# Transposing three of four normalised token groups by DMA, and running three partial products over twelve token blocks instead of eight

## The chip, the core and the metric

The kernel runs on one core of one Trainium2 chip. The time is that of the device for one execution, in microseconds, from runs without a profiler; the median of three was 243.69 (242.27 to 244.08). A profile is one separate execution, recorded by the hardware: its span goes from the first to the last instruction. Engines are named as in the profile: PE (TensorE; PEld are its weight loads), DVE (VectorE), ACT (ScalarE), POOL (GpSimd) and SP (SyncE, which here only issues DMAs). Each engine works through its own list of instructions in order, and an instruction that waits holds up all that stand behind it on the same engine.

## What is computed

```python
def _A_ref(x, wqkv, wo):                      # x: 1 x 2048 x 512
    # 32 heads of 16; every query sees itself and the 255 tokens before it
    ...
    scores = jnp.where(mask[None, None], scores, -1000000000.0)
    p = _softmax(scores, axis=-1)
    o = jnp.einsum('bhqk,bhkd->bhqd', p, v)
    return (lambda x, *d: x.transpose(*d))(o, 0, 2, 1, 3).reshape(B, S, D) @ wo

def _B_ref(x, w1, b1, w2, b2):                # mixes tokens: 2048 -> 1792 -> 2048
    h = _layernorm(x, axis=-1)
    u = jnp.einsum('bsd,sf->bdf', h, w1) + b1
    u = _gelu(u)
    y = jnp.einsum('bdf,fs->bds', u, w2) + b2
    return (lambda x, *d: x.transpose(*d))(y, 0, 2, 1)

mod = (_silu(c) @ w_mod).reshape(c.shape[0], 6, 1, -1)   # sa, ca, ga, sb, cb, gb
h = _layernorm(x, axis=-1) * (1 + ca) + sa
x = x + ga * _A_ref(h, A_wqkv, A_wo)
h = _layernorm(x, axis=-1) * (1 + cb) + sb
x = x + gb * _B_ref(h, B_w1, B_b1, B_w2, B_b2)
```

All tensors are bf16. The sums of the products are f32.

## The kernel before

The 2048 tokens are cut into 16 blocks of 128 (`tb`), and these into 4 groups of four blocks (`tg`). The program has three stretches.

**Attention.** A group's four blocks are normalised (`st1`, `e1`, `r1`, `ap1`: statistics, then `xn1`, 128 tokens x 512), turned so that the 512 channels lie on the partitions (tile `h1T`, 128 x 4 x 512 tokens), and scaled and shifted by the modulation on the way. From `h1T` PE makes K, Q and V (`Kk`, `Qq`, `V`; one of these is a group of four matmul steps with N = 512, cut into quadrants at some places). A slab `s` (0 to 15) is eight heads of one token group; its scores come in units (76 in all, `S0` to `S75`; four for each slab of the first token group, five for the others). PE computes a unit's scores into two PSUM tiles, and ACT takes the exponential of each tile (`E`, two for each unit, 152 in all, line 868). Then PE multiplies by V (`P`), DVE turns the result back (`turn`, line 899), POOL divides (`merge`, line 912) and DVE turns once more (`back`, line 921). `Wo` is the output projection, after which two layer norms (`s2` to `m2`, `s3` to `p3`) make `hb`, the input of the mixer, one tile for each token block.

**The mixer's first product.** It has 14 column chunks of 128 (`fc`), each a sum over the 16 token blocks. For the twelve chunks in `PART` the first eight blocks are summed during the attention, where PE has room between units (`B0` to `B11`, eight steps each), and the partial sum is copied to SBUF (`part`); the other eight blocks follow once the attention is over (`U`, eight steps; `A` adds the partial sum, `G` is the gelu on ACT). Chunks 12 and 13 do all sixteen steps in `U`. The weights `w1` of blocks 0 to 7 are loaded during the attention (tile `w1a`), those of blocks 8 to 15 when the attention's buffers have been released (`reopen`, tile `w1b`, eight DMAs).

**The mixer's second product** (line 1451) is a sum over the 14 chunks for each of the 16 output blocks, with its evictions and the stores of the output.

In the kernel before, a group is turned by PE: `T1`, `T2` and `T3` are two groups each of eight 128 x 128 transposes (line 1142) into a PSUM bank, and DVE evicts them with scale and shift (line 1155, four instructions for each token group). Token group 0 is turned by PE in both kernels (line 688).

What stands in which order on each engine is set by a planner in the kernel (class `Order`): it has a list of tasks with engine, estimated cost, dependencies and buffers, walks through time, and takes on each engine the ready task of lowest rank. The table `PLACES` shifts ranks task by task, `BY` says which engine does a task that several could do, and `PATIENCE` says how far PE may run a block of other work past the moment at which the next unit should start. A score unit needs two of three PSUM tiles, and everything else on PE shares two banks. All DMAs but two are issued from SP in one order; one DMA reuses the semaphore of the DMA that was issued eight earlier, and its issue waits until that one has landed.

Of the kernel before, what the change touches and what calls it, by code (L numbers as in the profile page):

```python
# [1501 lines left out]
```

## Time and profile before

| | |
|---|---|
| median of three runs | 243.69 us (242.27 to 244.08) |
| the profiled execution's own time | 242.86 us |
| its span, first to last instruction | 241.1 us |
| granted TensorE clock | 1.000 |
| matmul instructions on PE | 4316 |
| HBM read, written | 22.55 MB, 2.10 MB |
| mean DMA rate over the span | 117 GB/s |

The profiled execution took 0.83 us less than the median of the runs, and 1.76 us of its time lie outside the span. In the views that follow, a row of the timeline gives the start, the duration, the engine, the line, the operation, the output and its inputs, the count, and in brackets the engine's idle time before it and what ended that. Rows of equal instructions are merged, and a row can be one or two matmuls short. In a row of the windows the engines' busy times stand one after the other, each with its number of instructions, then the granted clock, the DMA engines' busy share and the rate.

### The profile page before, as it was taken

The numbers are of one execution on the slowest core, as the hardware profiler recorded it, in microseconds if no ns is written. First come the engines' busy times: TensorE is split into PE (matmuls) and PEld (weight loads), VectorE is DVE, ScalarE is ACT, GpSimd is POOL, SyncE is SP. The second block draws the span as 40 slices with busy tenths as digits, with TensorE's granted clock in tenths as the row PEclk, the third lists the DMA queues.
The fourth block names the chain that finished last, engine by engine and source line by source line (L and its number), as shares of the span: only waits on it lengthen the run. The fifth ranks groups of instructions, "written<-read, shape, count | busy, mean of one in ns | idle before, by whom it ended". The sixth has DMA issues, their size and how long they took to land.

```text
span 241.1 us, 9843 instructions
## 1 busy us (share of the span) xinstructions
PE 229.8 (95%) x4316; PEld 118.4 (49%) x4358; DVE 177.3 (74%) x422; ACT 162.0 (67%) x188; POOL 95.1 (39%) x148
## 2 busy tenths in 40 slices
PE   7899899999999999999999999999999999999994
PEld 2545546555555554454454455454444444444443
DVE  8899998878999899999356867989964306060644
ACT  7599989999999999999999999900436400000000
POOL 5219675741655466996310113686920000000000
PEclk9999999999999999999999999999999999999999
DMA  5998713062260343210110110059999001111121
GB/s 157 306 346 245 223 30 122 18 177 59 60 188 5 73 113 73 82 35 4 35 38 10 29 38 3 3 183 387 411 406 411 35 0 46 44 44 44 44 91 44
DMA packets 26151, 28.09 MB, mean 117 GB/s; under 512 B 10488, under 2 KB 23292, under 8 KB 26108
## 3 DMA queue, kind: packets, MB, share of 16 engines
q1 hardware_dynamic: 25956, 27.33, 36.0%
q8 instruction: 34, 0.56, 1.0%
q10 hardware_dynamic: 152, 0.13, 0.2%
q14 instruction: 9, 0.07, 0.1%
HBM read 22.55 MB, written 2.10 MB: 102 GB/s over the span
## 4 chain that ended last, share of the span: by engine, by line
PE 69%; DVE 16%; DMA 5%; issue 3%; SPq 3%; POOL 2%; ACT 1%; DVEq 0%; ACTq 0%
PE bk L606 17%; PE pss L1451 15%; PE bk L890 7%; PE pss L606 6%; PE pss L847 6%; PE bk L610 6%; PE bk L1451 5%; DVE stats L599 4%; DMA w1b<-in_B_w_dram 3%; DMA wqkv<-in_A_wqkv_dram 2%; DVE t L899 2%; PE pss L859 2%; PE pss L819 2%; PE pss L828 1%; DVE QR L740 1%
## 5 line engine op out<-in xcount | busy, mean ns | idle before, releaser
L868 ACT ACTIVATE et<-pss 128x1024 bf16<-128x1024 f32 x152 | 141.7, 1050 | 1.8 <-PE pss L859 1.6
L1451 PEld LDWEIGHTS <-w2r 128*128 128x128 bf16 x238 | 23.1, 98 | 25.6
L912 POOL TENSOR_TENSOR merge<-t,zr 128x512 bf16<-128x512 f32 x16 | 16.9, 1057 | 32.5 <-DVE zr L908 32.4
L1460 DVE SCALAR_TENSOR_TENSOR o<-pss,bFM,bc_gb 128x512 bf16<-128x512 f32 (+2 forms) x13 | 8.8, 705 | 27.9 <-PE pss L1451 27.9
L1451 PE MATMUL pss<-guT,w2r 128*128 128x512 bf16 (+2 forms) x128 | 28.1, 362 | 0.1
L899 DVE STREAM_TRANSPOSE t<-bk 128x512 f32<-128x512 f32 x32 | 22.6, 707 | 7.5 <-PE bk L890 7.3
L847 PE MATMUL pss<-QP,KT 32*128 32x64 bf16 (+2 forms) x672 | 24.2, 236 | 1.2 <-ACT et L868 0.2
L1048 POOL TENSOR_SCALAR QP<-QR,mask_par 128x512 bf16<-128x512 bf16 x22 | 15.0, 690 | 15.4 <-PE pss L859 6.2
L606 PE MATMUL bk<-hb,w1a 128*128 128x512 bf16 x76 | 19.9, 380 | 0.8 <-issue 0.5
L890 PE MATMUL bk<-et,V 128*32 128x256 bf16 (+2 forms) x704 | 19.2, 240 | 1.0 <-DVE t L899 0.3
L606 PE MATMUL pss<-hb,w1b 128*128 128x512 bf16 x80 | 19.9, 379 | 0.1
L847 PEld LDWEIGHTS <-KT 32*128 32x128 bf16 x672 | 11.1, 92 | 17.7 <-issue 14.8
L606 PE MATMUL bk<-h1T,wqkv 128*128 128x512 bf16 x67 | 18.8, 381 | 0.7 <-issue 0.2
L599 DVE BATCH_NORM_STATS2 stats<-x 128x6 f32<-128x512 bf16 x28 | 18.9, 674 | 0.2
L890 PEld LDWEIGHTS <-V 128*32 128x32 bf16 x704 | 15.2, 97 | 7.8 <-issue 3.3
L606 PEld LDWEIGHTS <-w1b 128*128 128x128 bf16 x112 | 10.9, 98 | 13.7 <-DMA w1b<-in_B_w_dram 0.6
L859 PE MATMUL pss<-mask_q,mask_k 32*128 32x256 bf16 x240 | 17.5, 268 | 0.0
L606 PE MATMUL bk<-wod,OT 128*128 128x512 bf16 x47 | 12.9, 380 | 0.4 <-DVE zr L908 0.2
L606 PEld LDWEIGHTS <-w1a 128*128 128x128 bf16 x90 | 7.9, 98 | 10.3 <-issue 2.5
L1255 DVE TENSOR_TENSOR x<-bk,x 128x512 bf16<-128x512 f32 x16 | 10.8, 675 | 2.8 <-PE bk L606 1.9
L921 DVE STREAM_TRANSPOSE OT<-merge 128x512 bf16<-128x512 bf16 x16 | 11.2, 699 | 2.0 <-POOL merge L912 1.8
L606 PE MATMUL bk<-wqkv,h1T 128*128 128x512 bf16 x40 | 12.0, 381 | 0.6 <-DVE stats L599 0.2
(144 smaller groups left out, 392.8 us busy)
## 6 DMA issues: line engine op xcount, KB each, us to landing
w2r<-in_B_w_dram SPq DMA_DIRECT2D x14, 512.0 KB, 10.4
w1a<-in_B_w_dram SPq DMA_DIRECT2D x16, 224.0 KB, 3.6
w1b<-in_B_w_dram SPq DMA_DIRECT2D x8, 448.0 KB, 6.9
wmod<-in_w_mod_dram SPq DMA_DIRECT2D x4, 512.0 KB, 7.2
x<-in_A_x_dram SPq DMA_DIRECT2D x15, 128.0 KB, 5.3
out_dram<-otile SPq DMA_DIRECT2D x15, 128.0 KB, 1.8
VL<-V SPq DMA_DIRECT2D x15, 96.0 KB, 2.3
wmod<-in_w_mod_dram SPq DMA_DIRECT2D x4, 256.0 KB, 4.3
```

Source lines behind the costliest of these rows:

```text
L599: nc.vector.bn_stats(out=stats[:], in_=src)
L606: nc.tensor.matmul(out[:], lhsT=lhsT, rhs=rhs, start=start, stop=stop, skip_group_check=True)
L610: nc.tensor.matmul(out[cols, :], lhsT=lhsT[:, cols], rhs=rhs, start=start, stop=stop, tile_position=(0, 32 * j), skip_group_check=True,)
L847: mm(pss[j // 2][:, j % 2, c0 : c0 + nq], lhsT=keys(4 * tg + kb)[rows[j], :], rhs=QP[s][rows[j], par, q0 : q0 + nq], start=n == 0, stop=False,
L859: mm(o, lhsT=mask_k[rows[j], 0:P], rhs=rhs, start=False, stop=True, tile_position=(32 * j, 0), skip_group_check=True,)
L868: nc.scalar.activation(out=et[:], in_=held.pop(("pss", u, a))[:], func=ACT.Exp, scale=SCORE_SCALE)
L890: nc.tensor.matmul(po[32 * j : 32 * j + 32, q0 : q0 + nq], lhsT=v(j), rhs=held["et", s, k, j // 2][:, j % 2, c0 : c0 + nq], start=n == 0, ...
L899: nc.vector.transpose(out=held["t2", s][:, par, :], in_=psum.pop(("po", s, par))[:])
L912: nc.gpsimd.tensor_tensor(out=m[:].rearrange("p (b a d) -> p a b d", a=2, d=DH), in0=t2v(s, 0, DH, DH), in1=held["zr", s][:].to_broadcast( ...
L921: nc.vector.transpose(out=OT[s][:], in_=held.pop(("m", s))[:])
L1048: engine[by(f"Qp{s}.{par}", "POOL")].tensor_scalar(out=QP[s][:, par, :], in0=QR[s][:], scalar1=mask_par[:, par : par + 1], scalar2=0.0, op ...
L1451: nc.tensor.matmul(py[:, lo:hi], lhsT=w2r[:, fc, tb * P : (tb + 1) * P], rhs=guT[fc][:, lo:hi], start=fc == made[0], stop=fc == made[-1], ...
```

## The change

Groups 1 to 3 are no longer turned by PE. For each of their blocks SP issues a DMA that transposes `xn1` from SBUF to SBUF into its quarter of `h1T` (`X`, twelve in all), and scale and shift are then applied in place in SBUF by DVE or POOL (`M`, one instruction for each 128 channels, twelve in all, seven on DVE and five on POOL). The products from `h1T` wait for all four `M` of their group.

Three of the twelve partial products, those of chunks 1, 6 and 11 (`LONG`), run over twelve token blocks, and their `U` over four. For that the `w1` rows of blocks 8 to 11 are loaded earlier: chunks 0 to 11 into the buffer of the projection weights `wqkv` once the last of K, Q and V has read it (`wx`), chunks 12 and 13 into a small tile of their own after the attention (`w1c`). What is left for `w1b` are four blocks instead of eight.

All tables of the planner are new, so nearly every instruction has another place in its engine's order. `PATIENCE` goes from 0.33 to 10.08.

```diff
-PATIENCE = 0.3286
+PATIENCE = 10.0775
 PART = (0, 1, 2, 3, 4, 5, 6, 7, 8, 9, 10, 11)
+LONG = (1, 6, 11)
...
-    'turn0.0': 4505.4, 'turn0.1': 4587.49, 'recip0': 4087.15, 'merge0': 4034.05, 'back0': 3614.07, 'turn1.0':
+    'turn0.0': 4320.49, 'turn0.1': 4319.51, 'recip0': 3683.47, 'merge0': 4131.76, 'back0': 3184.54, 'turn1.0':
...
-            return [] if tg == 0 else [f"T{tg}.0.", f"T{tg}.1."]
+            return [] if tg == 0 else [f"M{tg}.{dc}" for dc in range(ND)]
...
-                            nc.tensor.transpose(
-                                pt[:, n, tl * P : (tl + 1) * P], xn1[tg, tl][:, dc * P : (dc + 1) * P], identity[:]
-                            )
...
-                            nc.vector.tensor_scalar(
-                                out=h1T[tg][:, dc, :], in0=pt[:, n, :], scalar1=scale_of(dc), scalar2=shift_of(dc),
-                                op0=ALU.mult, op1=ALU.add,
-                            )
...
+            def open_h1(tg=tg):
+                h1T[tg] = hpool.tile([P, ND, 4 * P], DT.bfloat16, name="h1T")
+            add(f"h1.{tg}", "SP", 0.01, open_h1, lag=0.0, rank=rank + 1.5, deps=[f"r1.{tg}"], take=[("h1", tg)])
+            for tl in range(4):
+                def turned(tg=tg, tl=tl):
+                    dma.dma_start_transpose(out=h1T[tg][:, :, tl * P : (tl + 1) * P], in_=xn1[tg, tl][:])
+                add(
+                    f"X{tg}.{tl}", "SP", 0.65, turned, lag=3.0, rank=rank + 2 + tl * 0.1,
+                    deps=[f"ap1.{tg}.{tl}", f"h1.{tg}"], give=[("xn", (tg, tl))],
+                )
+            for dc in range(ND):
+                eng = by(f"M{tg}.{dc}", "DVE")
+
+                def modulate(tg=tg, dc=dc, eng=eng):
+                    h = h1T[tg][:, dc, :]
+                    engine[eng].tensor_scalar(
+                        out=h, in0=h, scalar1=scale_of(dc), scalar2=shift_of(dc), op0=ALU.mult, op1=ALU.add
+                    )
+                add(
+                    f"M{tg}.{dc}", eng, APPLY[eng], modulate, port=True, deps=[f"X{tg}.{tl}" for tl in range(4)],
+                    rank=rank + AHEAD["T"] + 0.1 * dc,
+                )
...
+        def begun(fc):
+            return 0 if fc not in PART else 12 if fc in LONG else 8
+
         def w1_of(sc, fc):
-            w = w1box["a"][:, sc, :] if sc < NA else w1box["b"][:, sc - NA, :]
-            return w[:, fc * P : (fc + 1) * P]
+            cols = slice(fc * P, (fc + 1) * P)
+            if sc < NA:
+                return w1box["a"][:, sc, cols]
+            if sc >= 12:
+                return w1box["b"][:, sc - 12, cols]
+            if fc < 12:
+                return wqkv[:, sc - NA, cols]
+            return w1box["c"][:, sc - NA, (fc - 12) * P : (fc - 11) * P]
+
+        add(
+            "wx", "SP", 0.66, lambda: dma.dma_start(out=wqkv[:], in_=w1_v[:, NA:12, 0 : 3 * D]), rank=550.0, lag=5.5,
+            deps=[f"V3.{tl}/3" for tl in range(4)] + [f"{k}{s}/3" for s in range(1, 16) for k in ("Kk", "Qq")],
+        )
...
-                dense_step(ps, w1_of(sc, fc), hb[sc][:], sc == 0, sc == 7)
+                dense_step(ps, w1_of(sc, fc), hb[sc][:], sc == 0, sc == begun(fc) - 1)
...
-            w1box["b"] = w1box["bpool"].tile([P, NT - NA, F], DT.bfloat16, name="w1b")
+            w1box["b"] = w1box["bpool"].tile([P, 4, F], DT.bfloat16, name="w1b")
+            w1box["c"] = w1box["bpool"].tile([P, 4, 2 * P], DT.bfloat16, name="w1c")
...
-            s0 = 8 if fc in PART else 0
+            s0 = begun(fc)
```

In the order lists below, ACT's `et` are the exponentials, `KT` the copies of K, `V` those of V and `part` those of the partial sums; on SP `VL` and `VU` are copies of V that the products `P` read, `xn` to `h1T` are the transposes, `x` the blocks of the input, `wod`, `wmod` and `b` weights and biases. First ACT before the change, from the first exponential on:

```order
L868 ACTIVATE et<-pss 128x1024 x4
L738 ACTIVATE V<-bk_484 128x16x2x16
L868 ACTIVATE et<-pss 128x1024 x2
L738 ACTIVATE V<-bk_554 128x16x2x16
L868 ACTIVATE et<-pss 128x1024 x2
L738 ACTIVATE KT_216<-bk_609 128x512
L868 ACTIVATE et<-pss 128x1024 x4
L738 ACTIVATE KT_216<-bk_780 128x512
L868 ACTIVATE et<-pss 128x1024 x140
```

And ACT after the change, over the same stretch to the last exponential:

```order
L874 ACTIVATE et<-pss 128x1024 x4
L744 ACTIVATE V<-bk_483 128x16x2x16
L874 ACTIVATE et<-pss 128x1024 x2
L744 ACTIVATE V<-bk_552 128x16x2x16
L874 ACTIVATE et<-pss 128x1024 x110
L744 ACTIVATE part_134<-bk_4123 128x512
L874 ACTIVATE et<-pss 128x1024 x20
L744 ACTIVATE part_136<-bk_4776 128x512
L874 ACTIVATE et<-pss 128x1024 x16
```

The two copies of K went to DVE, and two copies of partial sums came to ACT near the end of the attention; a third (`part_143`) follows the last exponential. Next SP before the change, where V's copies for slabs 1 and 2 are issued:

```order
L1006 DMA b_159<-in_B_b_dram 16x128
L1077 DMA VL_213<-V 64x4x192
L1083 DMA VU_215<-V 64x2x192
L1006 DMA wod<-in_A_wo_dram 128x4x512
L1006 DMA wmod<-in_w_mod_dram 128x4x512
L1006 DMA x_76<-in_A_x_dram 128x512
L1077 DMA VL_212<-V 64x4x192
L1083 DMA VU_214<-V 64x2x192
```

And SP after the change at the same place:

```order
L1083 DMA VL_213<-V 64x4x192
L1089 DMA VU_215<-V 64x2x192
L1146 DMA_TRANSPOSE h1T<-xn_657 128x4x128
L1146 DMA_TRANSPOSE h1T<-xn_637 128x4x128
L1146 DMA_TRANSPOSE h1T<-xn_610 128x4x128
L1146 DMA_TRANSPOSE h1T<-xn_775 128x4x128
L1012 DMA b_159<-in_B_b_dram 14x128
L1083 DMA VL_212<-V 64x4x192
L1089 DMA VU_214<-V 64x2x192
L1012 DMA x_75<-in_A_x_dram 128x512
L1012 DMA b_159<-in_B_b_dram 16x128
L1012 DMA wmod<-in_w_mod_dram 128x4x512
```

Group 1's four transposes stand between the copies of V for slab 1 and for slab 2. The load of `wod` now stands ahead of them, two of the four loads of `wmod` behind. Last DVE, where group 1 gets its scale and shift (`t` is `turn`, `zr` the reciprocal, `OT` is `back`, `n1ve` and `n1ng` are `e1` of another group). Before the change, from the reciprocal behind slab 0's second `turn` on:

```order
L908 RECIPROCAL zr<-t_729 128x32
L599 BN_STATS stats<-x_72 128x6
L600 BN_AGGR n1mv<-stats 128x2
L740 CAST QR<-bk_846 128x512
L1155 TENSOR_SCALAR h1T<-bk_862,modFM_93 128x512 x2
L571 TENSOR_SCALAR n1ve<-n1mv 128x4
L575 TENSOR_SCALAR n1ng<-n1mv 128x4
L1155 TENSOR_SCALAR h1T<-bk_900,modFM_94 128x512 x2
L899 STREAM_TRANSPOSE t_976<-bk_919 128x512
```

And DVE after the change, from slab 0's first `turn` on:

```order
L905 STREAM_TRANSPOSE t_779<-bk_659 128x512
L605 BN_STATS stats<-x_77 128x6
L606 BN_AGGR n1mv<-stats 128x2
L905 STREAM_TRANSPOSE t_779<-bk_729 128x512
L746 CAST KT_216<-bk_830 128x512
L914 RECIPROCAL zr<-t_779 128x32
L605 BN_STATS stats<-x_79 128x6
L606 BN_AGGR n1mv<-stats 128x2
L746 CAST KT_216<-bk_862 128x512
L927 STREAM_TRANSPOSE OT<-merge 128x512
L905 STREAM_TRANSPOSE t_992<-bk_890 128x512
L1156 TENSOR_SCALAR h1T<-h1T,modFM_93 128x512 x2
```

Before the change DVE evicted two PSUM tiles of transposes here, two instructions each. Now it takes on the two copies of K and applies scale and shift to half of `h1T` in place, while POOL does the other half.

More of the change, by code (lines that the diff above doesn't have):

```diff
@@ L42 @@
 PLACES = {
[75 rows of a table removed]
[79 rows of a table added]
 }
 BY = {
-    'Kk1.': 'DVE', 'Qq1.': 'DVE', 'Qp1.0': 'POOL', 'Qp1.1': 'DVE', 'Kk2.': 'ACT', 'Qq2.': 'DVE', 'Qp2.0':
-    'POOL', 'Qp2.1': 'POOL', 'Kk3.': 'ACT', 'Qq3.': 'DVE', 'Qp3.0': 'POOL', 'Qp3.1': 'POOL', 'Kk4.': 'DVE',
-    'Qq4.': 'DVE', 'Qp4.0': 'POOL', 'Qp4.1': 'POOL', 'Kk5.': 'DVE', 'Qq5.': 'DVE', 'Qp5.0': 'POOL', 'Qp5.1':
-    'POOL', 'Kk6.': 'DVE', 'Qq6.': 'DVE', 'Qp6.0': 'POOL', 'Qp6.1': 'POOL', 'Kk7.': 'DVE', 'Qq7.': 'DVE',
-    'Qp7.0': 'DVE', 'Qp7.1': 'POOL', 'Kk8.': 'DVE', 'Qq8.': 'DVE', 'Qp8.0': 'POOL', 'Qp8.1': 'POOL', 'Kk9.':
@@ L145 @@
-    'p3.15': 'DVE', 'B0.': 'DVE', 'B1.': 'DVE', 'B2.': 'DVE', 'B3.': 'DVE', 'B4.': 'DVE', 'B5.': 'DVE', 'B6.':
-    'DVE', 'B7.': 'DVE', 'B8.': 'DVE', 'B9.': 'DVE', 'B10.': 'DVE', 'B11.': 'DVE'
+    'Kk1.': 'DVE', 'Qq1.': 'DVE', 'Qp1.0': 'DVE', 'Qp1.1': 'DVE', 'Kk2.': 'DVE', 'Qq2.': 'DVE', 'Qp2.0': 'POOL',
+    'Qp2.1': 'POOL', 'Kk3.': 'DVE', 'Qq3.': 'DVE', 'Qp3.0': 'POOL', 'Qp3.1': 'POOL', 'Kk4.': 'DVE', 'Qq4.':
+    'DVE', 'Qp4.0': 'POOL', 'Qp4.1': 'DVE', 'Kk5.': 'DVE', 'Qq5.': 'DVE', 'Qp5.0': 'POOL', 'Qp5.1': 'POOL',
@@ new lines @@
+    'Kk6.': 'DVE', 'Qq6.': 'DVE', 'Qp6.0': 'DVE', 'Qp6.1': 'POOL', 'Kk7.': 'DVE', 'Qq7.': 'DVE', 'Qp7.0':
+    'POOL', 'Qp7.1': 'POOL', 'Kk8.': 'DVE', 'Qq8.': 'DVE', 'Qp8.0': 'POOL', 'Qp8.1': 'POOL', 'Kk9.': 'DVE',
+    'Qq9.': 'DVE', 'Qp9.0': 'POOL', 'Qp9.1': 'POOL', 'Kk10.': 'DVE', 'Qq10.': 'DVE', 'Qp10.0': 'POOL', 'Qp10.1':
+    'POOL', 'Kk11.': 'DVE', 'Qq11.': 'DVE', 'Qp11.0': 'DVE', 'Qp11.1': 'DVE', 'Kk12.': 'DVE', 'Qq12.': 'DVE',
+    'Qp12.0': 'DVE', 'Qp12.1': 'DVE', 'Kk13.': 'DVE', 'Qq13.': 'DVE', 'Qp13.0': 'DVE', 'Qp13.1': 'DVE', 'Kk14.':
@@ new lines @@
+    'DVE', 'Qq14.': 'DVE', 'Qp14.0': 'DVE', 'Qp14.1': 'POOL', 'Kk15.': 'DVE', 'Qq15.': 'DVE', 'Qp15.0': 'DVE',
+    'Qp15.1': 'POOL', 'V0.0.': 'ACT', 'V0.1.': 'DVE', 'V0.2.': 'ACT', 'V0.3.': 'DVE', 'V1.0.': 'DVE', 'V1.1.':
+    'DVE', 'V1.2.': 'DVE', 'V1.3.': 'DVE', 'V2.0.': 'DVE', 'V2.1.': 'DVE', 'V2.2.': 'DVE', 'V2.3.': 'DVE',
+    'V3.0.': 'DVE', 'V3.1.': 'DVE', 'V3.2.': 'DVE', 'V3.3.': 'DVE', 'ap1.1.0': 'POOL', 'ap1.1.1': 'POOL',
+    'ap1.1.2': 'DVE', 'ap1.1.3': 'DVE', 'M1.0': 'DVE', 'M1.1': 'DVE', 'M1.2': 'POOL', 'M1.3': 'POOL', 'ap1.2.0':
@@ L147 @@
+    'DVE', 'B4.': 'ACT', 'B5.': 'DVE', 'B6.': 'DVE', 'B7.': 'DVE', 'B8.': 'DVE', 'B9.': 'DVE', 'B10.': 'DVE',
+    'B11.': 'ACT'
 }
@@ L1275 @@
                 f"p2.{tb}", first_eng, APPLY[first_eng], p2, port=True, deps=[q], take=[("h2", tb)],
-                rank=rank + BEHIND["p2"] - (1e4 if first_eng == "ACT" else 0.0),
+                rank=rank + BEHIND["p2"],
             )
@@ L1292 @@
                 f"p3.{tb}", last_eng, APPLY[last_eng], p3, port=True, deps=[q], give=[("h2", tb)],
-                rank=rank + BEHIND["p3"] - (1e4 if last_eng == "ACT" else 0.0),
+                rank=rank + BEHIND["p3"],
             )
@@ L1331 @@
             group(
-                f"B{fc}", 8, mms, evac, act_cost=0.6, deps=[f"p3.{tb}" for tb in range(8)] + [f"w1.{n}" for n in range(2 * NA)],
+                f"B{fc}", begun(fc), mms, evac, act_cost=0.6,
+                deps=[f"p3.{tb}" for tb in range(begun(fc))] + [f"w1.{n}" for n in range(2 * NA)]
+                + (["wx"] if fc in LONG else []),
                 rank=1000.0 + n,
@@ L1409 @@
                     lambda key=key, i=i: held[key][:, i, :], [("pss", key)] if i == 0 else [], [("pss", key, ends)],
[L1410 removed]
+                    [f"U{f}/{NT - 1 - begun(f)}" for f in fcs],
                 )
```

56 lines of the change are left out of this document (18 added, 38 removed), and 170 rows, old and new, of tables (BY, PLACES).

## The prediction

> **What bounds the kernel now.** I read the busy times, then busy time by stretch, ACT's timeline, and PE's at the ends of the first stretch.
>
> ```profile
> PE 229.8 (95%) x4316; PEld 118.4 (49%) x4358; DVE 177.3 (74%) x422; ACT 162.0 (67%) x188; POOL 95.1 (39%) x148
> ...
> 32.30:156.82 124.52, 120.81 (x3362) 65.33 (x3394) 105.30 (x223) 124.32 (x134) 61.49 (x77) 1.00 0.23 58
> 157.10:189.43 32.33, 31.93 (x202) 14.76 (x198) 23.72 (x65) 10.40 (x15) 15.40 (x28) 1.00 0.89 342
> 189.43:238.00 48.57, 48.28 (x234) 23.00 (x237) 17.89 (x34) 1.33 (x2) 0.00 (x0) 1.00 0.13 41
> ```
>
> The shares of the whole span mix three limits. From 32.30 to 156.82 ACT is busy 124.32 of 124.52 us; PE is nearly as full, but here ACT sets the pace. From 157.10 to the end PE is busy all but 0.7 of 80.9 us: there only a matmul less makes the time less. The granted clock is 1.00 throughout.
>
> ```profile
> 19.16 2.00 ACT L868 ACTIVATE et<-pss 128x1024 bf16<-128x1024 f32 x2
> 20.96 0.68 ACT L738 ACTIVATE KT<-bk 128x512 bf16<-128x512 f32 x1
> 21.44 3.87 ACT L868 ACTIVATE et<-pss 128x1024 bf16<-128x1024 f32 x4
> 25.06 0.74 ACT L738 ACTIVATE KT<-bk 128x512 bf16<-128x512 f32 x1
> 25.54 5.77 ACT L868 ACTIVATE et<-pss 128x1024 bf16<-128x1024 f32 x6
> 32.30 124.52 ACT L868 ACTIVATE et<-pss 128x1024 bf16<-128x1024 f32 x134 [1.00 <-PE pss L859]
> ```
>
> 134 exponentials in 124.52 us are 0.929 each, with nothing between them: two for a unit, so a period of 1.858. The other 18 of 152 stand before 32.30, which makes the one at 32.30 that of unit S9, and S10's starts at 34.16 (32.30 + 2 x 0.929). Before that ACT loses 2 x 0.48 to copies of K (20.96 to 21.44, 25.06 to 25.54) and 1.00 waiting for S9.
>
> ```profile
> 28.58 0.98 DVE L1155 TENSOR_SCALAR h1T<-bk,modFM 128x512 bf16<-128x512 bf16 x2
> ...
> 29.62 1.05 PE L610 MATMUL bk<-wqkv,h1T 128*32 128x512 bf16 x16 [0.34 <-DVE h1T L1155]
> ...
> 31.70 0.40 PE L847 MATMUL pss<-QP,KT 32*128 32x256 bf16 x12
> ```
>
> That wait comes from the turning of group 1: the V product at 29.62 waits on PE for the second eviction of transposes, and S9 stands behind it and starts only at 31.70, 0.60 before its exponential.
>
> **The change, part by part.** *Tail.* Behind the last score unit PE's list holds 152 dense steps before (16 for `Wo`, 8 for `B3`, 128 for `U`) and 147 after (16, 15 for `B6` and `B11`, 116).
>
> ```profile
> 182.52 7.07 PE L606 MATMUL pss<-hb,w1b 128*128 128x512 bf16 x32
> 189.43 2.75 PE L1451 MATMUL pss<-guT,w2r 128*128 128x512 bf16 x11
> ```
>
> 32 steps take 6.91 us (182.52 to 189.43), 0.216 each, so five fewer are -1.08. Nothing else covers them, since PE idles nowhere there. The halved `w1b` load gives nothing more: PE did not stop for it. Ends: 0 (PE waits for late blocks instead) and -1.08.
>
> *ACT.* The two copies of K leave (-0.96); two copies of partial sums come at the same price (+0.96); a third lies behind the last exponential, where ACT has room (10.40 busy of 32.33). K's copies fall to DVE, below.
>
> *PE in the attention.*
>
> ```profile
> 26.30 0.61 PE L1142 MATMUL bk<-identity,xn 128*128 128x128 bf16 x8
> ```
>
> Six such groups go, at up to 0.61, and five steps come at 0.216: PE has up to 2.6 us less to do. Under ACT's pace that buys nothing by itself; the six evictions that DVE loses are in the next count.
>
> *Group 1, where the 1.00 can be won or lost.* In the new order S9 stands ahead of everything that reads group 1's `h1T`; the first reader is `Qq4`, behind S9 and ahead of S10. If ACT never waits, S4's first exponential starts at 20.96, twelve later S10's is due at 32.1, so S10 must start at 31.5. `Qq4` takes 0.98:
>
> ```profile
> 23.79 1.05 PE L610 MATMUL bk<-h1T,wqkv 128*32 128x512 bf16 x16
> 24.77 0.43 PE L819 MATMUL pss<-QP,KT 32*64 32x128 bf16 x32
> ```
>
> So all four `M1` must be done by 30.5. DVE has no idle time there, hence its list can be added up by start-to-start distances:
>
> ```profile
> 18.36 0.69 DVE L599 BATCH_NORM_STATS2 stats<-x 128x6 f32<-128x512 bf16 x1
> ...
> 19.18 0.32 DVE L1048 TENSOR_SCALAR QP<-QR,mask_par 128x512 bf16<-128x512 bf16 x1
> 19.44 0.69 DVE L599 BATCH_NORM_STATS2 stats<-x 128x6 f32<-128x512 bf16 x1
> ...
> 20.27 0.66 DVE L740 CAST V<-bk 128x512 bf16<-128x512 f32 x1
> 20.85 0.68 DVE L599 BATCH_NORM_STATS2 stats<-x 128x6 f32<-128x512 bf16 x1
> ...
> 24.45 0.68 DVE L899 STREAM_TRANSPOSE t<-bk 128x512 f32<-128x512 f32 x1
> 25.06 0.37 DVE L592 TENSOR_SCALAR xn<-x,n1r,n1sh 128x512 bf16<-128x512 bf16 x1
> 25.34 0.35 DVE L908 RECIPROCAL zr<-t 128x32 f32<-128x32 f32 x1
> ...
> 27.11 0.99 DVE L1155 TENSOR_SCALAR h1T<-bk,modFM 128x512 bf16<-128x512 bf16 x2
> ...
> 29.49 0.70 DVE L899 STREAM_TRANSPOSE t<-bk 128x512 f32<-128x512 f32 x1
> ```
>
> Statistics cost 0.82, a pad of Q 0.26, a cast 0.58, a `turn` or `back` 0.61, a normalisation 0.28. Up to its `M` pair the new list has, against the old one up to 29.49: one statistics less (-0.82), one pad, one normalisation, two casts, one `turn`, one `back` more (+0.26 + 0.28 + 1.16 + 1.22), and in place of 27.11 to 29.49 (-2.38) two `M`, which read and write SBUF as a normalisation does (+0.56). The sum is +0.28: DVE is done at 29.8, if it waits for nothing. POOL's pair takes 1.53:
>
> ```profile
> L592 POOL TENSOR_SCALAR xn<-x,n1r,n1sh 128x512 bf16<-128x512 bf16 x8 | 6.1, 765 | 1.2 <-PE bk L1142 1.0
> ```
>
> It must start by 29.0, and by then the last transpose must have landed. Its source comes from DVE at 18.36 + 3 x 0.82 + 2 x 0.26 + 3 x 0.58 + 2 x 0.28 = 23.6, the first transpose's source at 22.0 (one statistics, one cast and one normalisation earlier, 1.68). So the last has 5.4 us, the four together 7.0.
>
> *The transposes.* No row shows one. The nearest are the copies of V, SBUF to SBUF on the same queue, and the DMA load when they would run:
>
> ```profile
> L1077 SPq DMA_DIRECT2D VL<-V x15: 590/602/715, 21.0 to 140.6; - x15
> ...
> DMA to landing us min/median/max: 2.2/2.3/6.0
> ...
> 21.01 0.71 SPq L1077 DMA_DIRECT2D VL<-V  x1
> 21.77 0.60 SPq L1083 DMA_DIRECT2D VU<-V  x1
> ...
> 22.00:24.00 2.00, 1.94 (x104) 1.64 (x100) 1.97 (x5) 2.00 (x3) 2.00 (x4) 1.00 0.42 102
> 24.00:26.00 2.00, 1.95 (x58) 0.97 (x52) 1.97 (x6) 2.00 (x4) 0.83 (x2) 1.00 0.36 107
> ```
>
> SP spends 0.6 on an issue, and 96 KB land in 2.3 us when it is quiet, 6.0 behind large loads. About as many bytes stand ahead of the transposes as stood ahead of V's copy at 21.01, and from 22 on the DMA engines were under half busy. I take 3 us, near the quiet row since nothing large is queued: the last lands at 26.6, 2.4 early. Behind them SP's list has V's copies for slab 2 and two loads of `wmod`, delayed by 2.4 (4 x 0.6) at most, whose readers stand behind S11 and S13. Groups 2 and 3 have more room: group 2's buffer is free after `Qq7`, behind S20 (50.7 = 32.1 + 20 x 0.929), and DVE comes to its `M` behind S26 (61.8), so four transposes have 11 us. I take -0.7 of the 1.00, since DVE's margin is 0.7 and PE can slip in small waits; ends -1.0 and the first rival.
>
> *Late attention.* Five steps more lie ahead of the last unit, and `B1` there needs the norms of blocks 8 to 11, which before were needed only in the tail.
>
> ```profile
> 145.55 1.47 PE L606 MATMUL bk<-hb,w1a 128*128 128x512 bf16 x5
> 146.95 0.40 PE L847 MATMUL pss<-QP,KT 32*128 32x256 bf16 x8
> 147.38 0.61 PE L610 MATMUL bk<-hb,w1a 128*32 128x512 bf16 x8
> ```
>
> Six steps and a unit fill 1.83 us (145.55 to 147.38) of the period of 1.858, and the new order puts eight behind some units (S58, S68). ACT's two extra copies, 0.48 each, stand just there. I take +0.3; ends 0 and +1.1 (five steps returned).
>
> *Sum:* -0.7 - 1.08 + 0.3 = -1.5. The profiled execution's 242.86 becomes 241.4. It lay 0.83 under the median of the runs, 243.69, and against that the sum gives **242.2**.
>
> **Rivals.** *Transposes one after another (slower).* If they do not overlap and each takes issue and quiet landing, 0.6 + 2.3 = 2.9, four take 11.6: the last lands at 33.6, 4.6 late; group 2's are 0.6 late. All of it lies on PE's list ahead of S10 and of group 2's first V product, so ACT stands still: -1.0 + 4.6 + 0.6 - 1.08 = +3.1, **246.8**. It costs from 1.75 us apiece (7.0 / 4) and has eaten the gain of 2.1 at 2.3. For it: four back to back on one queue; against: V's second copy was issued 0.76 after its first, when that could not have landed (2.2 at least).
>
> *Transposes slow as well.* At the slowest row, 6.0 each in series, 24 us: 17 late for group 1, 13 for group 2, +28: **271.6**. The Trainium skill ("VectorE: DVE Perf Modes", The three transpose paths) lists 1309 ns for a 128x128 transpose by DMA against 390 ns on TensorE and advises TensorE where PSUM will do; four such blocks would be an estimated 5.2 us for each DMA and the sum 266. No run here shows that price; TensorE's eight took 0.61 us.
>
> *PE the bound at the end (no gain).* If units S58 to S74 are short of PE time or wait for the norms of blocks 8 to 11, the five steps return and such waits eat the early 0.7, 0.0: **243.7**. For it the 1.83 above; against, DVE's 105.30 of 124.52.
>
> *All of it (faster).* The 1.00 is won, and ACT's two late copies fall where ACT waits for PE anyway: -1.0 - 0.96 - 1.08 = -3.0, **240.7**.
>
> **How the numbers follow.** Forecast 0.46, serial transposes 0.22, PE the bound 0.14, all of it 0.14, slow transposes 0.04. The range from 240.6 to 247.2 leaves out the last, the serial case's upper third (0.08) and 0.06 below. Told from no change is about 1%, 2.4 us: faster means under 241.3, slower over 246.1. Faster: 0.12 of "all of it" and 0.12 of the forecast's lower side, 0.24. Slower: 0.18 of the serial case and 0.04, 0.22. The rest is 0.54.
>
> **What would show it.** In the profile after, ACT's exponentials run without a gap from 21 us, S10's starts at 32.1 to 32.5, the last ends near 156.1; the last step before line 1473 is about 1.5 us earlier than 189.43. A transpose should land within 3 us of its issue while others are on their way. I am wrong if `Qq4` waits on PE for `M1` by more than 1 us, if a gap in ACT shows between S20 and S28, or if PE idles at `B1` or `B6`.

## The result, and the profile after

The changed kernel takes 250.45 us (median of three; 249.51 to 251.48), the one before 243.26 in the same session: a ratio of 1.0298 with a 95% interval of 1.0226 to 1.0371. It is 3% slower, 8.25 us above the forecast of 242.2 and 3.25 above the upper end of the range, 247.2. A fourth execution took 379.6 us at a granted clock of 0.563; it, and one slower execution each of stats_later, copy_parts and loads_sp, stand outside all medians, ranges and ratios given here (the 250.9 from which one expectation below starts is the median with it). The profiled execution took 250.45 us, its span is 248.4 against 241.1 before.

The busy times of the page and the busy time by stretch, of after; the columns are those of the same rows before. First the page:

```profile
PE 233.9 (94%) x4277; PEld 116.7 (47%) x4277; DVE 175.3 (71%) x424; ACT 165.6 (67%) x191; POOL 94.1 (38%) x143
```

then the stretches:

```profile
33.00:165.40 132.40, 124.70 (x3347) 64.72 (x3340) 106.84 (x236) 124.67 (x135) 67.20 (x82) 0.99 0.33 84
165.40:197.00 31.60, 31.60 (x206) 14.57 (x195) 21.87 (x58) 12.61 (x18) 11.88 (x22) 1.00 0.78 300
```

From 33 us to the last exponential ACT is now busy 124.67 us of 132.40; before, the same stretch was 124.32 of 124.52. The exponentials are as many and as long as they were, and nearly 8 us of waiting have come between them. Behind the last exponential TensorE is still full. ACT's timeline of after shows where the waits lie:

```profile
21.75 11.49 ACT L874 ACTIVATE et<-pss 128x1024 bf16<-128x1024 f32 x12 [0.28 <-PE pss L865]
33.60 1.94 ACT L874 ACTIVATE et<-pss 128x1024 bf16<-128x1024 f32 x2 [0.36 <-PE pss L834]
38.77 1.94 ACT L874 ACTIVATE et<-pss 128x1024 bf16<-128x1024 f32 x2 [3.23 <-PE pss L865]
41.33 18.67 ACT L874 ACTIVATE et<-pss 128x1024 bf16<-128x1024 f32 x20 [0.63 <-PE pss L865]
60.61 20.45 ACT L874 ACTIVATE et<-pss 128x1024 bf16<-128x1024 f32 x22 [0.61 <-PE pss L865]
82.11 1.94 ACT L874 ACTIVATE et<-pss 128x1024 bf16<-128x1024 f32 x2 [1.05 <-PE pss L834]
84.72 1.94 ACT L874 ACTIVATE et<-pss 128x1024 bf16<-128x1024 f32 x2 [0.67 <-PE pss L865]
```

The largest, 3.23 us, is in group 1's place, a second cluster in group 3's. ACT waits for scores, so one has to look at what TensorE waited for. First the transposes: all twelve in one line with the time SP spent on an issue (min/median/max, ns), and their landing:

```profile
L1146 SPq DMA_TRANSPOSE h1T<-xn x12: 1195/1442/2257, 22.9 to 73.8; - x12
...
DMA to landing us min/median/max: 2.4/3.2/4.1
```

and SP's timeline at group 1:

```profile
22.89 6.58 SPq L1146 DMA_TRANSPOSE h1T<-xn  x4
29.53 0.61 SPq L1012 DMA_DIRECT2D b<-in_B_b_dram  x1
30.24 0.61 SPq L1083 DMA_DIRECT2D VL<-V  x1
30.94 0.59 SPq L1089 DMA_DIRECT2D VU<-V  x1
31.59 0.83 SPq L1012 DMA_DIRECT2D x<-in_A_x_dram  x1
```

They land about as I took it, 3.2 us behind their issue. But SP is held for 1.2 to 2.3 us by each, not 0.6, so the four of group 1 occupy it for 6.58 us, and the load of block 11 behind them is issued only at 31.59. VectorE's and TensorE's timelines of after, at that place:

```profile
30.74 1.12 DVE L1156 TENSOR_SCALAR h1T<-h1T,modFM 128x512 bf16<-128x512 bf16 x2 [0.17 <-DMA h1T<-xn]
34.14 0.69 DVE L605 BATCH_NORM_STATS2 stats<-x 128x6 f32<-128x512 bf16 x1 [2.28 <-DMA x<-in_A_x_dram]
...
35.70 0.17 PE L1175 MATMUL bk<-identity,b 30*128 30x30 bf16 x1 [2.12 <-DVE t L905]
36.28 1.27 PE L612 MATMUL bk<-wqkv,h1T 128*128 128x512 bf16 x4 [0.41 <-DVE QR L746]
```

VectorE's two modulations are done at 31.9, 1.4 later than the prediction had allowed for `Qq4`. Then VectorE stands for 2.28 us before the statistics of block 11, which belong to group 2 and are not used until four units later; `turn1.1` and `Qq4`'s copy stand behind them on VectorE, and TensorE waits for both. And the idle time is paid for twice. TensorE in stretches of 1 us, with the granted clock third from the right:

```profile
36.00:37.00 1.00, 0.72 (x4) 0.36 (x4) 1.00 (x4) 0.00 (x0) 0.68 (x2) 0.96 1.06 374
37.00:38.00 1.00, 1.00 (x7) 0.16 (x9) 0.72 (x3) 0.00 (x0) 1.00 (x2) 0.50 1.14 337
38.00:39.00 1.00, 1.00 (x20) 0.49 (x23) 1.00 (x4) 0.23 (x1) 0.60 (x2) 0.50 0.41 82
39.00:40.00 1.00, 1.00 (x16) 0.39 (x12) 0.04 (x1) 1.00 (x2) 0.82 (x3) 0.50 0.01 4
40.00:41.00 1.00, 1.00 (x52) 0.68 (x44) 0.81 (x2) 0.70 (x1) 0.59 (x1) 0.83 0.05 16
41.00:42.00 1.00, 1.00 (x24) 0.44 (x20) 1.00 (x2) 0.67 (x1) 0.00 (x0) 1.00 0.14 28
```

After waits of 2.12 and 0.41 us the clock is halved from 36.9 to about 40.3, which is another 1.7 us of TensorE's time. The Trainium skill ("TensorE: Matmul & The Clock Gate", Part 1: The HAM clock gate) gives half the clock as the idle state and about 3.4 us of sustained work to leave it; the 3.4 us at 0.50 agree.

At group 3, SP, GpSimd and TensorE of after:

```profile
68.71 3.61 SPq L1146 DMA_TRANSPOSE h1T<-xn  x2
...
73.83 1.25 SPq L1146 DMA_TRANSPOSE h1T<-xn  x1
...
78.09 0.77 POOL L1156 TENSOR_SCALAR h1T<-h1T,modFM 128x512 bf16<-128x512 bf16 x1 [3.92 <-issue]
...
79.98 1.46 PE L612 MATMUL bk<-wqkv,h1T 128*128 128x512 bf16 x6 [1.12 <-DVE KT L746]
```

The last transpose of group 3 is issued at 73.83 and lands near 78; GpSimd, in its turn with a modulation of that group, stands for 3.92 us with `Qp8`'s pads behind it.

**A ledger.** ACT's 152 exponentials are a clock for the whole middle of the kernel. I count them along ACT's timeline and read off when the 1st, 25th, 97th and 152nd start (inside a row they are spaced evenly). Before: 12.73, 37.87, 104.74, 155.82, and the span ends at 241.1. Each column is a stretch's length less that of before, in us, for one profiled execution; the row adds up to the difference of the spans.

| kernel | to 1st | 1st to 25th (group 1) | 25th to 97th (groups 2, 3) | 97th to 152nd (late attention) | 152nd to the end | span |
|---|---|---|---|---|---|---|
| after | +0.3 | +3.2 | +3.3 | +1.8 | -1.3 | 248.4 |
| stats_later | +0.1 | +0.1 | +6.1 | +1.5 | -1.2 | 247.7 |
| both_later | +0.5 | +3.2 | +1.8 | +1.5 | -1.3 | 246.9 |
| plain_copy | +0.6 | -1.6 | +2.4 | +1.8 | -1.2 | 243.1 |
| copy_parts | +0.2 | +6.2 | +2.7 | +1.5 | -1.0 | 250.7 |
| sp_order | +0.7 | +4.6 | +1.7 | +1.5 | -1.2 | 248.3 |
| group_x | 0.0 | -1.0 | +3.9 | +1.7 | -1.4 | 244.3 |
| loads_first | +2.0 | +0.8 | +3.6 | +1.8 | -1.2 | 248.0 |
| loads_sp | +0.7 | -0.4 | +2.7 | +1.5 | -1.2 | 244.3 |
| group_loads | -0.2 | -1.2 | +2.4 | +1.4 | -1.4 | 242.2 |
| group_loads_dve | +0.3 | -1.2 | +2.6 | +1.9 | -1.4 | 243.3 |
| no_long | +0.4 | +3.2 | +4.6 | +2.0 | +2.9 | 254.2 |

### The profile page after: what moved, and what is told of

Same layout as the page of the kernel before. It is cut to its first block, busy times and chain, and to the rows that moved or that the text cites. A ratio compares the mean times of both kernels' runs of the same rounds, so it can differ in the third digit from the quotient of the medians.

```text
span 248.4 us, 9744 instructions
## 1 busy us (share of the span) xinstructions
PE 233.9 (94%) x4277; PEld 116.7 (47%) x4277; DVE 175.3 (71%) x424; ACT 165.6 (67%) x191; POOL 94.1 (38%) x143
## 4 chain that ended last, share of the span: by engine, by line
PE 79%; DVE 7%; issue 3%; DMA 3%; SPq 3%; ACT 2%; POOL 1%; ACTq 0%
PE bk L612 26%; PE pss L1473 15%; PE pss L612 7%; PE bk L896 7%; PE pss L853 6%; PE bk L616 6%; PE bk L1473 5%; DMA x<-in_A_x_dram 3%; PE pss L825 2%; PE pss L865 2%; ACT et L874 2%; DVE stats L605 2%; PE pss L834 2%; SPq L448 2%; DVE x L1252 1%
## 5 line engine op out<-in xcount | busy, mean ns | idle before, releaser
L612 PE MATMUL bk<-h1T,wqkv 128*128 128x512 bf16 x88 | 23.3, 383 | 1.4 <-DVE h1T L1156 0.9
L612 PEld LDWEIGHTS <-wqkv 128*128 128x128 bf16 x128 | 11.6, 98 | 16.6 <-issue 5.1
L1054 POOL TENSOR_SCALAR QP<-QR,mask_par 128x512 bf16<-128x512 bf16 x18 | 12.8, 717 | 13.0 <-DVE QR L746 7.2
L612 PE MATMUL bk<-wqkv,h1T 128*128 128x512 bf16 x55 | 14.8, 385 | 2.1 <-DVE KT L746 1.1
L612 PEld LDWEIGHTS <-w1a 128*128 128x128 bf16 x97 | 8.5, 98 | 11.1 <-issue 2.4
L896 PE MATMUL bk<-et,VL 128*32 128x64 bf16 x512 | 12.1, 193 | 0.4 <-issue 0.4
L612 PE MATMUL bk<-wod,OT 128*128 128x512 bf16 x50 | 12.3, 380 | 0.2 <-DVE x L1252 0.2
```

The source lines that it names most:

```text
L612: nc.tensor.matmul(out[:], lhsT=lhsT, rhs=rhs, start=start, stop=stop, skip_group_check=True)
L896: nc.tensor.matmul(po[32 * j : 32 * j + 32, q0 : q0 + nq], lhsT=v(j), rhs=held["et", s, k, j // 2][:, j % 2, c0 : c0 + nq], start=n == 0, ...
L1054: engine[by(f"Qp{s}.{par}", "POOL")].tensor_scalar(out=QP[s][:, par, :], in0=QR[s][:], scalar1=mask_par[:, par : par + 1], scalar2=0.0, op ...
```

## The experiments

Each median is of three to five executions; ratios are to the kernel before on the same chip. After itself stands at 250.45 and 1.0298. After was measured in another session than the experiments, so gains against it are good to some tenths of a microsecond at best. Where the planner's list is kept and single steps are put elsewhere in it, this is the helper, and the diffs show its calls:

```diff
         order.go(PATIENCE)
+        def move(name, ahead_of):
+            names = [x[3] for x in order.log]
+            task = order.log.pop(names.index(name))
+            names.remove(name)
+            order.log.insert(names.index(ahead_of), task)
```

### stats_later: VectorE's wait alone

```diff
+        move("st1.2.3", "st1.2.2")
```

> Only VectorE's statistics of block 11 (they wait 2.28 us for that block's load, which SP issues behind four transposes) go from ahead of turn1.1 to ahead of the statistics of block 10; SP's order is that of the changed kernel. Theory 1 (SP's issues hold back what is queued behind them, and VectorE's order passes it on): the 3.23 us that ACT idles before the exp at 38.77 shrink to at most 1.2, the granted clock of the stretch from 33 to 42 us goes from 0.81 to above 0.95, and the time goes from 250.5 to 246.0 (245 to 247.5). Theory 2 (the transposes land late, so TensorE waits for group 1's modulation whatever VectorE does): the gap stays above 2.5 and the time above 249. Theory 3 (the clock falls by itself under the new order): the gap shrinks, but the clock stays near 0.8 and the time at 247.5 to 249.

Measured: 249.69 us (248.53 to 252.23), ratio 1.0281 (1.0209 to 1.0353); 246.0 was expected. The step went as theory 1 said, the time did not. In the profiled execution group 1's 3.2 us are gone (+0.1 in the ledger) and the clock from 33 to 42 us is 1.00. But TensorE then stops at the next load in the same jam, the bias `b`, and later for group 2:

```profile
34.36 0.17 PE L1175 MATMUL bk<-identity,b 30*128 30x30 bf16 x1 [1.17 <-DMA b<-in_B_b_dram]
...
67.71 0.62 PE L616 MATMUL bk<-h1T,wqkv 128*32 128x512 bf16 x4 [1.55 <-POOL h1T L1156]
```

Group 2's last transpose took 5.0 us to land there, and the clock fell to 0.72 from 66 to 72 us. Taking one waiter out of the jam leaves the jam.

### both_later: and two modulations of group 3

```diff
+        move("st1.2.3", "st1.2.2")
+        move("M3.1", "k2.2")
+        move("M3.3", "Qq11.")
```

> The move of stats_later, and two modulations of group 3 go later: the one on GpSimd, which kept it idle 3.92 us, from ahead of Qp8.0's pads to ahead of k2.2, the last one on VectorE (1.04 us of waiting) to ahead of Qq11's copy; what uses group 3 comes only three units after that. Theory 1: the second loss goes too, ACT's two gaps before the exps at 82.11 and 84.72 (1.05 and 0.67) fall to 0.3 each, and the time is 1.5 us under that of stats_later: 244.5 (243 to 246). Rival (TensorE is late there with its own work, since group 2's and 3's products crowd in those units): the gaps move a unit or two later and the time is within 0.5 of stats_later.

Measured: 249.78 us (248.97 to 250.48), ratio 1.0264 (1.0234 to 1.0295); 244.5 was expected. The gaps of group 3 went (0.17 at most where 1.05 and 0.67 stood). Group 1, though, lost its 3.2 us again, by the road of theory 2. SP and TensorE of both_later:

```profile
22.82 7.36 SPq L1146 DMA_TRANSPOSE h1T<-xn  x4
...
34.15 1.87 PE L612 MATMUL bk<-h1T,wqkv 128*128 128x512 bf16 x4 [3.32 <-DVE h1T L1156]
```

Here the four issues held SP for 7.36 us, the modulation began at 33.0, and TensorE waited for it directly. My two theories were two results of one cause: SP held for 6.6 to 7.4 us makes group 1 itself late and everything queued behind it too, and which of them is the last differs from one profiled execution to the next: both kernels have the same order at group 1, and stats_later lost 0.1 there, both_later 3.2.

### plain_copy: the same bytes, not turned

```diff
-                    dma.dma_start_transpose(out=h1T[tg][:, :, tl * P : (tl + 1) * P], in_=xn1[tg, tl][:])
+                    dma.dma_start(
+                        out=h1T[tg][:, :, tl * P : (tl + 1) * P],
+                        in_=xn1[tg, tl][:].rearrange("p (c k) -> p c k", c=ND),
+                    )
```

> The 12 transposes are plain copies of the same bytes from SBUF to SBUF, in the same order on SP; it leaves out the transposition, so the products of groups 1 to 3 are of other numbers. Theory 1 (what costs is the transposing DMA, its issue above all): an issue takes 0.7 us or less instead of 1.2 to 2.26, the modulation of group 1 is done before 30.5 instead of 32.4, VectorE waits less than 0.5 for block 11's load, and the time is 243.5 (242 to 245). Rival (the new order itself costs: the modulation in SBUF on VectorE and GpSimd, the late placing of attention, the 12-block part products): the time stays above 248.

Measured: 244.69 us (244.61 to 245.07), ratio 1.0059 (1.0042 to 1.0077): 5.8 us off the changed kernel, which bears out theory 1 and leaves 1.4 us to the new order. The issue and the landing in plain_copy:

```profile
L1146 SPq DMA_DIRECT2D h1T<-xn x12: 599/613/1277, 22.9 to 68.0; - x12
...
DMA to landing us min/median/max: 2.3/3.0/4.0
```

and SP's and VectorE's timelines of plain_copy at group 1:

```profile
22.91 3.13 SPq L1146 DMA_DIRECT2D h1T<-xn  x4
...
30.67 0.69 DVE L1159 TENSOR_SCALAR h1T<-h1T,modFM 128x512 bf16<-128x512 bf16 x2
```

The landing is that of the transposes (2.4/3.2/4.1); the issue differs, 613 ns against 1442 in the median, and SP is held for 3.13 us instead of 6.58. Group 1's stretch is now 1.6 shorter than before the change. The modulation was not done before 30.5, as expected, but only at 31.4, since VectorE's own list had not come to it sooner; that did no harm.

### copy_parts: the issue time put back

```diff
+                    ends = (0, 1, 2, ND) if tg == 1 else (0, 2, ND)
+                    for a, b in zip(ends, ends[1:]):
+                        dma.dma_start(
+                            out=h1T[tg][:, a:b, tl * P : (tl + 1) * P],
+                            in_=xn1[tg, tl][:, a * P : b * P].rearrange("p (c k) -> p c k", c=b - a),
+                        )
```

> As plain_copy (the transposition is left out, the same bytes are copied), but each block's copy is cut into three in group 1 and into two in groups 2 and 3, so that SP spends about 3 x 0.61 = 1.8 and 2 x 0.61 = 1.2 us a block, as with the transposes (1.65 and 1.2 to 1.9), with nothing turned. Theory 1 (the time SP takes to issue is the cause): the gaps come back, group 1's modulation starts after 31.5 us and the time is 250 (248.5 to 251.5). Rival (turning itself costs: the transfer, or what it does to other transfers): the time stays at plain_copy's 244.7 (244 to 246).

Measured: 252.44 us (250.66 to 253.36), ratio 1.0366 (1.0314 to 1.0418); 250 (248.5 to 251.5) was expected. With nothing turned the whole loss is back, and more than that, for SP is held longer than by the transposes. The issues of copy_parts, and SP's timeline at group 1:

```profile
L1148 SPq DMA_DIRECT2D h1T<-xn x28: 513/614/1858, 22.5 to 78.2; - x28
...
22.49 9.92 SPq L1148 DMA_DIRECT2D h1T<-xn  x12
```

and ACT's gaps at group 1:

```profile
37.10 1.94 ACT L874 ACTIVATE et<-pss 128x1024 bf16<-128x1024 f32 x2 [4.41 <-PE pss L834]
42.08 1.94 ACT L874 ACTIVATE et<-pss 128x1024 bf16<-128x1024 f32 x2 [3.05 <-PE pss L865]
```

The twelve copies hold SP for 9.92 us, not for the 7.2 that was planned, so the run does not repeat the transposes' time exactly. But plain_copy, after and copy_parts have the same order on every engine, and group 1's stretch follows the time that SP is held there: -1.6 at 3.13 us, +3.2 at 6.58, +6.2 at 9.92. That settles the cause at group 1: SP's time for the issues, not the turning and not the transfer.

### sp_order: groups 2 and 3

```diff
+        move("h1.2", "h1.3")
+        move("X2.1", "VLU4")
+        move("X2.2", "VLU4")
+        move("X2.3", "w1.0")
+        move("X2.0", "w1.0")
+        for tl in (0, 2, 1, 3):
+            move(f"ap1.3.{tl}", "turn4.1")
+        for x in ("h1.3", "X3.0", "X3.2", "X3.1", "X3.3"):
+            move(x, "w1.2")
```

> The changed kernel with group 2's tile taken ahead of group 3's, so that two of group 2's transposes go ahead of V's copies for slab 4 and the other two ahead of the first load of w1 (they stood from 56.7 to 64.3 us, though their blocks were normalised by 48), and group 3's blocks and transposes go ahead of the third load of w1. Group 1 is as it was. Theory 1: ACT's gaps between 58 and 90 us (0.61, 1.05 and 0.67, together 2.3 with what is under 0.3) go to under 0.8, group 1's gaps stay; 250.5 - 1.6 = 248.9 (247.5 to 250). Rival (groups 2 and 3 have room anyway, and what the later gaps show is TensorE catching up after group 1): within 0.7 of the changed kernel.

Measured: 249.68 us (248.44 to 250.32), ratio 1.0258 (1.0226 to 1.029): 0.8 less, where theory 1 expected 1.6 and the rival at most 0.7. In the profile the stretch of groups 2 and 3 loses 1.7 instead of 3.3, with no gap over 0.53; group 1 lost more than in after (4.6, VectorE again 3.06 us before block 11). The intervals of this kernel and of after overlap, so the time decides nothing; what speaks for theory 1 is the ledger. With after's order in this stretch it shows +3.3, +3.6 and +4.6 (after, loads_first, no_long; stats_later, with a halved clock besides, +6.1), with the new order +1.7 and +2.7 (sp_order, loads_sp). The first three also say how far one execution differs from the next: by 1.3 us.

### group_x: one wide transpose

Here a group's four blocks are written into one tile, ordered by column block first, so that its 2048 columns come out in the order of `h1T`.

```diff
-                    dma.dma_start_transpose(out=h1T[tg][:, :, tl * P : (tl + 1) * P], in_=xn1[tg, tl][:])
+                    left[tg] -= 1
+                    if not left[tg]:
+                        dma.dma_start_transpose(
+                            out=h1T[tg][:].rearrange("k c (t p) -> k (c t) p", t=4),
+                            in_=xn1[tg][:].rearrange("p c t k -> p (c t k)"),
+                        )
```

> sp_order's order, with a group's four normalised blocks in one tile and one transpose of 128x2048 for the group instead of four of 128x512; the same result. Theory 1a (an issue costs SP a fixed time): SP is busy at most 3 us a group instead of 5.6 to 8.4, group 1's modulation starts by 29.5, the load of block 11 is issued by 28.5, and the time is 244.5 (243 to 246). Theory 1b (an issue costs by what it turns): the one issue takes 4.5 us or more, group 1 lands at 32 or later since it now waits for all four blocks, and the time is no better than sp_order's (248 to 252).

Measured: 246.63 us (245.74 to 247.93), ratio 1.015 (1.0107 to 1.0192): 3 us under sp_order, 2 above what 1a gave. Issue and landing in group_x:

```profile
L1154 SPq DMA_TRANSPOSE h1T<-xn x3: 1939/2035/2055, 24.3 to 57.7; - x3
...
DMA to landing us min/median/max: 5.6/5.7/5.9
```

and SP's timeline there:

```profile
24.35 2.04 SPq L1154 DMA_TRANSPOSE h1T<-xn  x1
...
28.89 0.59 SPq L1013 DMA_DIRECT2D x<-in_A_x_dram  x1
```

Four times the data cost SP 2.04 us, 0.6 more than a narrow transpose in the median: the issue is mostly a fixed price. 1a was wrong on the landing: 5.7 us in the median, so the modulation starts at 30.3, no earlier than in sp_order (30.6). Yet group 1 loses nothing, which points to the loads behind: block 11's goes out 2.7 us earlier than in after. In groups 2 and 3 it loses 3.9, and why is not shown.

### loads_first, loads_sp, group_loads, group_loads_dve

Three loads go ahead of the transposes: alone, with sp_order's moves, with group_x, and there with two copies of part products taken off ACT.

```diff
+        for x in ("L.b1", "L.b2", "L.x11"):
+            move(x, "VLU1")
```

> The changed kernel with three loads (the two biases and block 11, 1.6 us of SP) moved on SP from behind group 1's four transposes to ahead of V's copies for slab 1, where SP stands idle from 18.2 to 21.2 us; nothing else moves, and the transposes themselves keep their times. Theory 1, narrowed (not group 1's landing, but the loads queued behind the transposes cost the time, since VectorE's statistics wait for block 11 and TensorE's bias transpose for b): neither waits any more, the exp that came at 41.33 comes at 37.5 (37 to 38.6), the granted clock from 33 to 42 us is above 0.95, and the time is 3.5 less: 247.4 (246 to 248.5). Theory 2 (group 1 lands late, and TensorE waits for it): that exp stays at 40 or later and the time above 249.

> loads_first and sp_order together: the loads ahead of group 1's transposes, group 2's and 3's transposes earlier on SP; twelve transposes of 128x512 as in the changed kernel. Theory: the two losses lie at different places, so both gains add: 250.9 - 3.5 - 1.3 = 246.1 (244.8 to 247.3). Rival (one loss seen twice: what is saved early is waited for later): within 0.5 of loads_first.

> group_x with the three loads ahead of group 1's transpose as in loads_first. Theory: group_x had lost nothing in group 1 any more (its exp of the same number came at 36.88), because SP was through with the transposes 3 us earlier; so nothing is left to gain there: 246.6 (245.8 to 247.4), as group_x. Rival (the wide transpose gained by something else, and the loads still hold up VectorE or TensorE): 245.3 or less.

```diff
+        BY.update({"B2.": "DVE", "B4.": "DVE"})
```

> group_loads with the copies of two part products (B2 and B4, 0.6 us each on ACT in the midst of the exps) on VectorE, as in the kernel before. Theory (ACT with its exps sets the pace there): 2 x 0.6 = 1.2 less, 245.4 (244.6 to 246.2). Rival (TensorE or VectorE sets it, VectorE's copies take 0.69 each): no change, 246.6.

Measured: loads_first 248.5 us (247.1 to 250.19), ratio 1.0196 (1.0145 to 1.0247); loads_sp 245.74 (245.48 to 246.32), 1.0107 (1.0065 to 1.0148); group_loads 245.43 (244.2 to 246.72), 1.0107 (1.0052 to 1.0162); group_loads_dve 245.67 (245.12 to 246.46), 1.0102 (1.0061 to 1.0143).

loads_first gained 2.0 of the expected 3.5. Neither VectorE nor TensorE waits for a load any more. Its profiled execution, the longest of the four, had its first exponential 1.7 us later than after's (the clock was 0.57 from 11 to 15 us); counted from there group 1 loses 0.8. What is left is the group's own lateness, which no load can cure, on VectorE and TensorE of loads_first:

```profile
32.69 1.12 DVE L1156 TENSOR_SCALAR h1T<-h1T,modFM 128x512 bf16<-128x512 bf16 x2 [0.73 <-DMA h1T<-xn]
...
33.86 1.02 PE L612 MATMUL bk<-h1T,wqkv 128*128 128x512 bf16 x3 [1.42 <-DVE h1T L1156]
```

So the clock from 33 to 42 us still fell to 0.81, against the expectation. loads_sp came out as expected, 250.45 - 245.74 = 4.7 under after, which speaks against the rival of one loss seen twice. It is more than the 2.0 and 0.8 that the two moves gave alone, so that the gains just add is not shown. group_loads lies 1.2 under group_x and below its expected range, close to the rival's 245.3; the intervals overlap. Its ledger shows group 1 as good as unchanged, as expected, and the difference in groups 2 and 3, whose order is the same in both, so this stays undecided. group_loads_dve gained nothing. The windows from the 97th to the 152nd exponential, first of group_loads, then of group_loads_dve:

```profile
105.79:158.29 52.50, 50.16 (x1363) 26.12 (x1377) 38.79 (x91) 52.26 (x58) 21.03 (x27) 1.00 0.20 57
```

```profile
106.43:159.39 52.96, 50.20 (x1363) 26.17 (x1378) 39.86 (x93) 51.72 (x56) 21.43 (x27) 1.00 0.20 57
```

Spared the two copies, ACT is idle for 1.24 us instead of 0.24, and the stretch gets no shorter; 0.9 of its waits from 106 to 160 us were for TensorE. None of the four beats the kernel before.

### no_long: the 12-block parts alone

```diff
-LONG = (1, 6, 11)
+LONG = ()
```

> LONG is empty: no part product runs over 12 blocks, all 12 stop at 8; transposes by DMA and the layout of w1 stay. By the planner's count 153 steps instead of 149 of TensorE then stand behind the last unit of scores. Theory (my term for the end: each step that moves ahead of the last unit saves its 0.216 us): 4 x 0.216 = 0.9 us slower than the changed kernel, 251.4 (250.7 to 252). Rival (the end is not bound by TensorE's steps): within 0.3 of the changed kernel, 250.5; ahead of the last exp nothing changes in either case (it ends at 165.4).

Measured: 253.79 us (252.6 to 256.2), ratio 1.0405 (1.0376 to 1.0435): 3.3 slower than after (2.6 by the ratios), not 0.9. With `LONG` empty the planner also places other steps anew from the late attention on, so the edit is not the long parts alone. The profiled execution was the slowest of the five, 256.2 us; in its ledger the end is 4.2 longer than after's. TensorE ran out of steps before the last blocks were normalised; its timeline of no_long:

```profile
183.41 0.38 PE L612 MATMUL bk<-hb,w1b 128*128 128x512 bf16 x1 [2.17 <-ACT hb L594]
```

and the window behind, with the granted clock third from the right:

```profile
185.00:190.00 5.00, 5.00 (x18) 1.94 (x17) 1.62 (x7) 1.25 (x1) 2.62 (x6) 0.71 1.03 410
```

In after TensorE does not stop there; it is busy for all of the 35.00 us from 160 to 195. Four steps are 0.9, the wait 2.2, and the clock at 0.71 for 5 us another 1.4: together 4.5, near the 4.2.

## Why the prediction was wrong

Put into the columns of the ledger, the prediction's terms are -1.66 for group 1 (-0.7, and -0.96 for the copies of K that leave ACT), 0 for groups 2 and 3, +1.26 for late attention (+0.3, and +0.96 for the copies of partial sums that come to ACT) and -1.08 for the end. After shows +3.2, +3.3, +1.8 and -1.3.

**The step that failed** is the price of the transposes, in two sentences of it. "SP spends 0.6 on an issue" was read off copies of V; a transpose of 128x512 costs SP 1.2 to 2.3. "I take 3 us ... the last lands at 26.6" would have held for the transfer (3.2 in the median), but SP was not through with the fourth before 29.5 (22.89 + 6.58), and the modulation could start only at 30.7, where it had to be done by 30.5. I bounded the transfer from both sides and the issue from none. In the profile of after the late landing itself is the smaller part: VectorE's own list came to the modulation only at 30.6 (29.2 in my sum, the 29.8 less 0.56; a wait of 0.46 for TensorE's product of K is in it), and `Qq4` waited for `M1` for 0.86, less than the 1 us that I had named as the sign of being wrong. The larger part came from what stood behind the transposes on SP.

**"Behind them SP's list has V's copies for slab 2 and two loads of `wmod`, delayed by 2.4"**: the list was short by the two biases and block 11, and the delay was 6.58. Block 11's statistics are not due for four units; but they stand on VectorE ahead of `Qq4`'s copy, and an engine that works in order passes a wait on to all behind it. I asked whose readers are urgent and not where they stand.

**"Groups 2 and 3 have more room ... 11 us"**: group 2's transposes stood on SP from 56.73 to 64.2, the last of them behind a load of `w1`, and group 3's until 75.1 for a modulation on GpSimd planned before that. The stretch lost 3.3; putting the transposes earlier gave back 1.6 of it, plain copies 0.9. I had put this stretch at nothing, and SP's time explains only a part of what it lost.

**The rival of serial transposes** (246.8, 0.22) had the sign and the place, but the wrong mechanism: they do overlap in flight, with SP held for about 1.65 us by each (6.58 / 4) and landings in 2.4 to 4.1. It also priced a late group 1 once, where the halved clock added 1.7. The Trainium skill ("VectorE: DVE Perf Modes", The three transpose paths), by whose 1309 ns a block I had estimated 5.2 for each DMA, is not borne out in the price: 4.1 at most for four blocks in after (5.0 in stats_later), 5.9 for sixteen. Its advice to transpose on TensorE has this much for it: no kernel here with DMA transposes beat the one before, though none turns these groups on TensorE in the new order.

**Group 1's -0.7** was a fair size for what I had priced: with SP's issues at 0.6 (plain_copy) the stretch is 1.6 shorter than before, against the -1.66 above.

**The tail's -1.08** was right: -1.25 in after, -1.0 to -1.4 in all kernels with the long parts. In no_long's one profile the end lost more without the long parts than their four steps come to.

**Late attention**, +1.26 by the column (2.06 with the upper end of +1.1), came to +1.8, and to between 1.4 and 2.0 in every variant, so it lies inside what I had allowed. ACT's two copies and TensorE's five steps were both candidates. Without the copies (group_loads_dve) the stretch shows +1.9, and ACT then waits for TensorE, which speaks for the rival that TensorE is the bound at the end; but with four of the steps moved behind the last unit (no_long) it still shows +2.0. Neither alone is shown to be the cause.

**What stays open.** In the stretch of groups 2 and 3 every variant still loses 1.7 us or more (2.4 in plain_copy and group_loads, in waits of ACT of 0.2 to 1.0 us for TensorE); I did not trace it to one cause. In plain_copy TensorE is busy 66.39 of 69.26 us there, against 64.86 of 66.87 before, though I had given it less to do. Giving group 1 alone back to TensorE, and an order planned with the true price of an issue (the planner has 0.65 us for a transpose), were not tried on the chip.

## What to carry to other kernels

A DMA has two prices, its landing and the time it holds the queue that issues it. Bound both, and when the second is not on the page, list everything behind it on that queue and, for each reader, what is queued behind the reader on its own engine. If transposes must go by DMA, make them wide and put the loads that others wait for in front.
